# A long convolution whose first transform stage is cut into 32-column groups and turned on chip

## Chip, cores and metric

The kernel runs on one core of one Trainium2 chip. The metric is the device time of one execution in microseconds (us); smaller is better. Three runs of the kernel before gave 924.21 us as their median (921.7 to 927.91). A core has five engines with queues of their own: TensorE (PE in the profile, its weight loads PEld), VectorE (DVE), ScalarE (ACT), GpSimd (POOL) and SyncE (SP), which here issues nearly all DMA transfers. Everything is float32.

## What is computed

```python
def _attn_ref(x, h):                      # x (8, 5696, 128), h (5696, 128)
    L = 2 * S
    Xf = np.fft.rfft(x, n=L, axis=1)
    Hf = np.fft.rfft(h, n=L, axis=0)
    return np.fft.irfft(Xf * Hf[None], n=L, axis=1)[:, :S, :]

def _moe_ref(x, phi, w1, w2):             # x (45568, 128): the result above, flattened
    logits = x @ phi                      # 32 slots: 8 experts of 4
    d = np.exp(logits - logits.max(0)); d /= d.sum(0) + 1e-09
    slot_input = (d.T @ x).reshape(E, S_per_e, D)
    slot_out[e] = np.maximum(slot_input[e] @ w1[e], 0) @ w2[e]       # for each e
    c = np.exp(logits - logits.max(1, keepdims=True)); c /= c.sum(1, keepdims=True) + 1e-09
    return c @ slot_out.reshape(n_slots, D)
```

First a long causal convolution of each of eight sequences with one filter h, channel by channel; then a layer of soft slots, whose slot inputs are weighted over all 45,568 tokens, so that no output row can be written before all tokens are through the convolution.

## The kernel before

The convolution is a transform of length 5760 = 90 x 64 (N1 = 90, N2 = 64) in two stages, a product with the filter's transform, and two stages back. "Image" g = 0 is the filter h, images 1 to 8 are the sequences.

**Stage A** (`load_x`, `fold`, `stage_a`). An image is read in eight chunks of 2 x 4 of the 64 residues. GpSimd folds a chunk with its mirror into a sum and a difference (L201); each of these is multiplied by two tables (L212: 128 columns, of which 90 are used, by 512), ScalarE copies the product out of PSUM into `fst` (L214), and two DMAs store it in DRAM as F (L218), 1 KB per run. That is 32 products per image.

**Stage B** (`load_g`, `stage_b1`, `stage_b2`). The second stage needs the 64 residues on the partitions, so F is loaded back turned (`gt`, L236). A unit is up to four frequencies of each half: 8 matmuls of 64x64 weights by 256 columns, both parts of 128 channels (L250), into `bt`; two multiplications by the filter's transform, Hr and Hi (L270; for h itself by the table `turn`, and the result becomes Hr, Hi); a sum and a difference (L279, on VectorE, in some steps one on GpSimd); `stage_b2` takes the way back (L294), ScalarE copies (L299), and a DMA stores z in DRAM (L302), 1 KB per run. There are 12 units per image: 11 full ones and one with a single frequency of each half.

**Stage C**, per pair T, four of them per image, 32 in all. `load_pair` loads a quarter of an image's z (`zc`, one buffer, two DMAs, L330). `stage_c1` makes the last transform stage: four products of two 64-column matmuls each (L349), ScalarE copies the odd ones, VectorE forms sums and differences (`fold_out`, L354 and L355), GpSimd the last four (`after`, L368). `stage_c2` transposes the 16 blocks (L377), `stage_c3` makes the logits (L386), `column_max` a running maximum per slot (L397 to L405), `stage_c4` transposes the logits and takes the row maximum (L415 to L431), `stage_c5` transposes the exponentials (L438), `softmax` normalises the rows, `dispatch` adds to the slot inputs `acc` (L462, L467), and `stage_c6` stores the weights for the end (`c_t`).

**Order.** The order is written out by hand; the loop at L563 runs over steps t of one chunk of A each. B runs LAG_B = 9 steps behind A, C another 18 behind B, a pair every second step, its parts spread over five steps. Every engine takes its instructions in the order in which this loop issues them. The short-lived products of A and C share a ring of four PSUM banks (L154); `bt` and `bz` have two banks each. When the last unit of B is out, the front's memory is freed and a second loop (L696) finishes the pairs that are left (27 on), with w1 and w2 loaded beside it. Then come the experts (L764 to L794) and the output, eight images in three groups each (L819 to L836).

Of the kernel before, what the change touches and what calls it, by code (L numbers as in the profile page):

```python
# [10 lines left out]
F32 = mybir.dt.float32  # L11
# [3 lines left out]
PSUM = bass.MemoryType.PSUM  # L15

# [6 lines left out]
def transform_tables(S, N1, N2, CH, X0, F0, F1):  # L23

# [4 lines left out]
    N, R1, HALF, P = N1 * N2, S // N2, N2 // 2, 2 * N2  # L36
    k1 = np.arange(N1)
# [3 lines left out]
    s1 = np.stack([np.cos(a1), -np.sin(a1), -np.cos(a1)], 1)  # L41
    a0 = np.outer(alpha, np.arange(N1 // 2) + 0.5)
    i1 = np.stack([np.cos(a0), -np.sin(a0), -np.cos(a0)], 1)
    NP = N1 // 2
    part = s1
    s1 = np.zeros((P, 3, P))
    for a, p in enumerate((F0, F1)):
        s1[X0:X0 + R1, :, p:p + NP] = part[:, :, a * NP:(a + 1) * NP]
    part = i1[np.arange(N1).reshape(2, NP).T.reshape(-1)]
    i1 = np.zeros((P, 3, N2))  # L50
    for r, n, p in z_blocks(N1):
        i1[p:p + n, :, 0:NP] = part[r:r + n]
# [3 lines left out]
    a2 = m2[None, :, None] * omega[:, None, :]  # L56
    w = np.concatenate([np.cos(a2), np.sin(a2)], 1)
    back = np.arange(N2).reshape(2, HALF // CH, CH).transpose(1, 0, 2).reshape(-1)
    NU = (NP + 1) // 2
    turn = (N1 - 1) / 2 * alpha[:, None] + (N2 - 1) / 2 * omega  # L60
    wq = np.zeros((2, N2, NP, N2))
    vq = np.zeros((2, N2, NU, 2, N2))
    tn = np.zeros((2, N2, 2, (NU + 1) // 2, 2, 2))
    for a in range(2):
        wq[a] = w[a * NP:(a + 1) * NP].transpose(1, 0, 2)
        for q in range(NP):
            vq[q % 2, :, q // 2, a] = w[a * NP + q][back].T
            tn[q % 2, :, 0, q // 4, a, q // 2 % 2] = np.cos(turn[a * NP + q]) / N
            tn[q % 2, :, 1, q // 4, a, q // 2 % 2] = np.sin(turn[a * NP + q]) / N
    wq, vq, tn = [t.reshape(P, *t.shape[2:]) for t in (wq, vq, tn)]  # L70
    return [np.ascontiguousarray(t, dtype=np.float32) for t in (s1, i1, wq, vq, tn)]
# [3 lines left out]
def kernel(  # L75
# [13 lines left out]

# [11 lines left out]
    NU = (NP + 1) // 2  # L111
    NW = (NU + 1) // 2
# [4 lines left out]
    NQ = NJ // 2  # L117
    assert S == R1 * N2 and R1 == N1 - 1 and D == P and CH == Q == 4
    SPLIT = R1 // 16 * 16
    X0, F0, F1 = 20, 6, 82  # L120
    ctx.enter_context(tc.manual_schedule())

    t_s1, t_i1, t_w, t_v, t_turn = [
        nc.inline_tensor(t, f"tab_{n}").ap()
        for n, t in zip(("s1", "i1", "w", "v", "turn"), transform_tables(S, N1, N2, CH, X0, F0, F1))]
    fd = [nc.dram_tensor(f"f_{g}", (2, N2, NP, 2, D), F32, kind="Internal").ap() for g in range(B + 1)]
    zd = [nc.dram_tensor(f"z_{b}", (NP, 2 * N2, 2, D), F32, kind="Internal").ap() for b in range(B)]
# [26 lines left out]
    rings = [mid.enter_context(tc.tile_pool(name="ps", bufs=4, space=PSUM))]  # L154
    bps = front.enter_context(tc.tile_pool(name="bps", bufs=1, space=PSUM))
    fconst = front.enter_context(tc.tile_pool(name="fconst", bufs=1))
    lead = ExitStack()
    apool = lead.enter_context(tc.tile_pool(name="apool", bufs=2, side="right"))
    bpool = front.enter_context(tc.tile_pool(name="bpool", bufs=1))

    s1 = apool.tile([P, 3, P], F32, name="s1", tag="s1", bufs=1)
    wt = fconst.tile([P, NP, HP], F32, name="wt")
    vt = fconst.tile([P, NU, 2, HP], F32, name="vt")
    turn = fconst.tile([P, 2, NW, 2, 2], F32, name="turn")
    Hr = fconst.tile([P, NW, 2, 2, D], F32, name="Hr")
    Hi = fconst.tile([P, NW, 2, 2, D], F32, name="Hi")

    def bank():
        rings.append(rings.pop(0))
        return rings[-1].tile([P, 512], F32, name="bank", tag="bank")  # L170
# [5 lines left out]
    for t_ in xcs:  # L176
        nc.vector.memset(t_[:, :, :, :], 0.0)

    def load_x(c):
        if c >= (B + 1) * NJ:  # L180
            return
        g, j = divmod(c, NJ)
# [683 lines left out]
```

## Time and profile before

| | us |
|---|---|
| runs: median (lowest to highest) | 924.21 (921.7 to 927.91) |
| profiled execution, its span | 922.1 |
| VectorE's first and last addition to `acc` (L467) begin at | 237.0, 843.3 |
| first and last product on `zc` (L349) begin at | 182.6, 817.5 |
| SP's issues of x (L190), first and last of the sequences, at | 33.8, 643.7 |

| group | busy us | times |
|---|---|---|
| PE L212, stage A | 275.9 | 576 records, 288 products |
| PE L250, L294, stage B | 116.4, 104.9 | 1620, 1440 records |
| PE L349, stage C1 | 117.1 | 480 records |
| DVE L270 (full, by Hr and by Hi) | 107.4, 106.9 | 88, 88 |
| DVE L279 (full) | 141.4 | 150 |
| ACT L214, copies of stage A | 171.9 | 288 |
| POOL L201, folds | 192.8 | 144 |

DMA moved 272.45 MB in 156,552 packets, 295 GB/s as a mean; 288 stores of F of 180 KB and 99 + 9 loads of F of 512 and 128 KB are among them.

How to read it: busy time counts an engine's instructions without issue or waiting, "records" are the instructions of a group as the profiler lists them (a float32 product is two). Times of matmuls are modelled at their ends, so spacings of their starts say more than their lengths. In the rows, out<-in name what is written and read, the number after "x" is a count, and after the bar stand the busy time in all, the mean of one in ns, and idle time before the group with what ended it.

### The profile page before, as it was taken

What the parts mean: (1) busy time and instruction counts of PE and PEld (TensorE: products, weight loads), DVE (VectorE), ACT (ScalarE), POOL (GpSimd) and SP (SyncE); (2) the same over time, 40 slices, a digit from 0 to 9 for tenths busy, and PEclk for the clock granted to TensorE, in tenths of its full rate; (3) what the DMA queues carried; (4) which work ended last, traced back from release to release, by engine and by line L of the source; (5) the groups of instructions that cost most, each with busy time, mean ns of one, the idle gap of its engine ahead of it and who ended that gap; (6) DMA issues with size and microseconds to landing.
All of it is one profiled execution on the core that took longest, in us unless ns stands there. A gap on an engine that the chain in (4) does not pass through costs nothing.

```text
span 922.1 us, 19325 instructions
## 1 busy us (share of the span) xinstructions
PE 818.0 (89%) x7220; PEld 423.9 (46%) x7220; DVE 653.1 (71%) x887; ACT 481.7 (52%) x888; POOL 488.1 (53%) x426
## 2 busy tenths in 40 slices
PE   6968898899999999999999999999987777878893
PEld 2323344345444445544554454444444434345783
DVE  3047665478888878888888788988887775674552
ACT  4623454455556655555666666656553344475442
POOL 4648766546655565556565655655466552472000
PEclk9989999899999999999999999999999888798865
DMA  9989999999899999999999999999989887761798
GB/s 298 279 274 299 272 345 311 289 345 327 268 320 319 314 282 324 316 314 285 341 304 327 289 324 329 297 318 320 316 269 330 272 254 198 211 249 73 272 405 341
DMA packets 156552, 272.45 MB, mean 295 GB/s; under 512 B 11766, under 2 KB 114422, under 8 KB 153317
## 3 DMA queue, kind: packets, MB, share of 16 engines
q1 hardware_dynamic: 155883, 270.85, 91.4%
q8 instruction: 58, 0.95, 0.4%
q10 hardware_dynamic: 576, 0.36, 0.2%
q14 instruction: 35, 0.29, 0.1%
HBM read 142.86 MB, written 128.21 MB: 294 GB/s over the span
## 4 chain that ended last, share of the span: by engine, by line
PE 51%; DMA 31%; POOL 5%; DVE 5%; issue 3%; SPq 2%; ACT 2%; DVEq 0%; POOLq 0%; ACTq 0%
PE bank L212 17%; DMA zc<-z 11%; PE bank L349 9%; DMA gt<-f 8%; PE bt L250 7%; PE bz L294 6%; DMA out_dram<-o 4%; PE bank L377 4%; DVE p L270 2%; POOL y L368 2%; DMA f<-fst 2%; PE bank L462 2%; DMA z<-zst 2%; PE bank L438 2%; PE bank L386 2%
## 5 line engine op out<-in xcount | busy, mean ns | idle before, releaser
L212 PE MATMUL bank<-x,s 128*128 128x512 f32 x576 | 275.9, 614 | 12.3 <-POOL x L201 12.0
L201 POOL TENSOR_TENSOR x<-xc 128x512 f32<-128x512 f32 x144 | 192.8, 1342 | 154.7 <-PE bank L212 70.4
L214 ACT ACTIVATE fst<-bank 128x512 f32<-128x512 f32 x288 | 171.9, 597 | 95.5 <-PE bank L212 74.8
L299 ACT ACTIVATE zst<-bz 128x1024 f32<-128x1024 f32 x96 | 93.2, 971 | 205.4 <-PE bz L294 198.5
L270 DVE TENSOR_TENSOR p<-bt,Hr 128x1024 f32<-128x1024 f32 x96 | 112.9, 1176 | 108.0 <-PE bt L250 95.7
L212 PEld LDWEIGHTS bank<-x,s 128*128 128x128 f32 x576 | 102.4, 193 | 131.5 <-issue 93.4
L279 DVE TENSOR_TENSOR yf<-p 128x512 f32<-128x512 f32 (+1 forms) x163 | 146.4, 931 | 3.3
L250 PE MATMUL bt<-gt,wt 64*64 64x256 f32 x1620 | 116.4, 394 | 25.1 <-DMA gt<-f 22.0
L349 PE MATMUL bank<-zc,i 128*64 128x512 f32 x480 | 117.1, 610 | 7.0 <-DMA zc<-z 4.1
L294 PE MATMUL bz<-yf,vt 64*64 64x256 f32 x1440 | 104.9, 393 | 15.5 <-POOL yf L279 15.0
L270 DVE TENSOR_TENSOR p<-bt,Hi 128x1024 f32<-128x1024 f32 x96 | 112.3, 1170 | 0.0
L250 PEld LDWEIGHTS bt<-gt,wt 64*64 64x64 f32 x1620 | 55.0, 134 | 102.0 <-issue 31.6
L368 POOL TENSOR_TENSOR y<-y,op 128x512 f32<-128x512 f32 x64 | 77.5, 1211 | 7.8 <-DVE op L354 5.1
L294 PEld LDWEIGHTS bz<-yf,vt 64*64 64x64 f32 x1440 | 58.2, 137 | 44.2 <-POOL yf L279 21.0
L279 POOL TENSOR_TENSOR yf<-p 128x512 f32<-128x512 f32 (+1 forms) x29 | 45.9, 1583 | 53.9 <-DVE p L270 53.9
L368 POOL TENSOR_TENSOR y<-y,om 128x512 f32<-128x512 f32 x54 | 71.8, 1330 | 2.1
L270 DVE TENSOR_TENSOR p<-bt,turn 128x1024 f32<-128x1024 f32 (+1 forms) x24 | 27.2, 1174 | 57.8 <-PE bt L250 57.7
L349 PEld LDWEIGHTS bank<-zc,i 128*64 128x64 f32 x480 | 30.8, 138 | 68.3 <-issue 40.8
L377 PE MATMUL bank<-ident,y 109*128 109x109 f32 x512 | 60.0, 275 | 0.7 <-DVE y L368 0.7
L377 PEld LDWEIGHTS bank<-ident,y 109*128 109x128 f32 x512 | 53.5, 151 | 13.6 <-issue 11.9
L379 ACT ACTIVATE yt<-bank 128x360 f32<-128x360 f32 x128 | 50.9, 482 | 3.3 <-PE bank L377 3.3
L819 PE MATMUL op<-so,cT 32*128 32x128 f32 x704 | 46.0, 374 | 4.4 <-ACT o L828 3.6
(97 smaller groups left out, 851.5 us busy)
## 6 DMA issues: line engine op xcount, KB each, us to landing
f<-fst SPq DMA_DIRECT2D x288, 180.0 KB
gt<-f SPq DMA_DIRECT2D x99, 512.0 KB
z<-zst SPq DMA_DIRECT2D x88, 512.0 KB
zc<-z SPq DMA_DIRECT2D x30, 1024.0 KB
xc<-in_x_dram SPq DMA_DIRECT2D x64, 320.0 KB
out_dram<-o SPq DMA_DIRECT2D x16, 1024.0 KB
zc<-z SPq DMA_DIRECT2D x30, 416.0 KB
out_dram<-o SPq DMA_DIRECT2D x8, 768.0 KB
```

Of the source, the lines that this page charges most:

```text
L201: nc.gpsimd.tensor_tensor(out=y_[:, :, :], in0=t_[:, 0, :, :], in1=t_[:, 1, ::-1, :], op=AL.subtract if comp else AL.add)
L212: nc.tensor.matmul(p[:, :], s1[:, tab[G], :], src[:, :, :].rearrange("p n d -> p (n d)"), start=True, stop=True)
L214: nc.scalar.activation(st[:, :, G, :], p[:, :].rearrange("p (n d) -> p n d", d=D), AF.Copy)
L250: nc.tensor.matmul(bt[q * HP:(q + 1) * HP, a, o, :], wt[r, 2 * i + q, :], t_[r, 2 * o + q, :, :].rearrange("p c d -> p (c d)"), start=True ...
L270: nc.vector.tensor_tensor(out=p_[r, 0:k, :, :], in0=pv, in1=h_, op=AL.mult)
L279: eng.tensor_tensor(out=y_[r, 0:k, c, :], in0=pr[r, 0:k, c, :], in1=pi[r, 0:k, 1 - c, :], op=op_)
L294: nc.tensor.matmul(bz[a * HP:(a + 1) * HP, q, o, :], vt[r, i, a, :], y_[r, a * m + o, :, :].rearrange("p c d -> p (c d)"), start=True, sto ...
L299: nc.scalar.activation(st[:, 0:m, 0:n, :].rearrange("p o q x -> p q o x"), bz[:, 0:n, 0:m, :], AF.Copy)
L349: nc.tensor.matmul(p[h_ * HP:(h_ + 1) * HP, :], i1[0:kr, tab, :], t_[0:kr, h_, o, :, q, :], start=True, stop=True)
L368: eng.tensor_tensor(out=part_, in0=part(v, 0), in1=o_[:, :, :], op=sign)
L377: nc.tensor.transpose(p[:, i * TR:(i + 1) * TR], ys[T][0:TR, k * CH + i, 0:D], ident[0:TR, 0:TR])
L379: nc.scalar.activation(yt[:, k * CH:(k + 1) * CH, :, :], of_tokens(p), AF.Copy)
```

## The change

The first stage leaves no F in DRAM, and half of the channels (64) are worked on at a time; there are 18 such halves H, nine images of two. A half is loaded as eight DMAs into one tile X[dh] of two, with 256 bytes per run. GpSimd folds it in place, in four steps j of two operations.

`stage_a(H, k)` makes eight products: 32 columns of the table each, by 32 residues x 16 channels, in two groups of four that write the four 32-partition quarters of one tile `pa` (two PSUM banks, one buffer). Table columns are ordered so that a quarter holds 32 frequencies of one kind (even or odd below 64 for k = 0 to 3, the 26 others for k = 4, 5) and one part. VectorE then turns `pa` by one transposition of 32x32 blocks into F1 or F3, which have the residues on the partitions, and `stage_b1` reads them at once.

A half has six units of stage B: four of 16 matmuls of 128 columns, one of 32 and one of 20 of 64 columns. The two multiplications now write `pi` and, in place, `bt` in PSUM, and both sums are on VectorE, with one operand in `bt`. `bt`, `bz`, `pa` and `pi` have one buffer each. z is stored in runs of 512 bytes.

In stage C the parts are placed by unit: a pair takes three units (STARTS), with `stage_c1` cut in two. Its PSUM ring has two banks while the front runs, eight after it. The running maximum is one reduction, since ScalarE no longer overwrites the unused column, which holds LOWEST; the difference of maxima goes into the exponential as its bias. The front now holds 28 pairs, so the closing loop begins at pair 28. Tables change with the layout.

```diff
@@ memory
-    rings = [mid.enter_context(tc.tile_pool(name="ps", bufs=4, space=PSUM))]
+    banks = [front.enter_context(tc.tile_pool(name="ps", bufs=2, space=PSUM))]
+    aps = front.enter_context(tc.tile_pool(name="aps", bufs=1, space=PSUM))
     bps = front.enter_context(tc.tile_pool(name="bps", bufs=1, space=PSUM))
...
+    F1 = bpool.tile([P, 32, 2, HD], F32, name="F1")
+    F3 = bpool.tile([P, 32, 2, 32], F32, name="F3")
+    X = [apool.tile([P, N2 + 8, HD], F32, name=f"X{i}") for i in range(2)]
+    NH = 2 * (B + 1)
@@ loading and folding
+        for n0 in (0, 48, 16, 32):
+            for r in (slice(0, SPLIT), slice(SPLIT, R1)):
+                nc.sync.dma_start(out=X[dh][r, 8 + n0:24 + n0, :],
+                                  in_=src[r, n0:n0 + 16, dh * HD:(dh + 1) * HD])
...
+        for op_, dst in ((AL.add, t_[0:R1, 8 * j:8 * j + 8, :]),
+                         (AL.subtract, t_[0:R1, hi:hi - 8:-1, :])):
+            nc.gpsimd.tensor_tensor(out=dst, in0=t_[0:R1, lo:lo + 8, :],
+                                    in1=t_[0:R1, hi:hi - 8:-1, :], op=op_)
@@ stage A
-            nc.scalar.activation(st[:, :, G, :],
-                                 p[:, :].rearrange("p (n d) -> p n d", d=D), AF.Copy)
-            nc.sync.dma_start(
-                out=fd[g][a, n0:n0 + CH, :, :, :].rearrange("n q c d -> q n (c d)"),
-                in_=st[p:p + NP, :, :, :].rearrange("k n c d -> k n (c d)"))
...
+        p = aps.tile([P, 2, 512], F32, name="pa", tag="pa")
+        for c in range(2):
+            for q in range(4):
+                a, comp = divmod(q, 2)
+                d0 = 16 * k if k < 4 else 16 * (k - 4) + 32 * a
+                nc.tensor.matmul(p[32 * q:32 * q + 32, c, :],
+                                 s1[0:R1, comp + c, a if k < 4 else 2, :],
+                                 t_[0:R1, 40 * comp:40 * comp + 32, d0:d0 + 16],
+                                 start=True, stop=True)
+        def turn():
+            f_ = F1[:, :, :, 16 * k:16 * k + 16] if k < 4 else \
+                F3[:, :, :, 16 * (k - 4):16 * (k - 4) + 16]
+            nc.vector.transpose(f_.rearrange("p k c d -> p c d k"),
+                                p[:, :, :].rearrange("p c (n d) -> p c d n", d=16))
@@ stage B
+        o0, no = (0, 4) if i < 4 else (0, 8) if i == 4 else (8, 5)
+        for o in range(no):
+            for a in range(2):
+                r = slice(a * HP, (a + 1) * HP)
+                for par in range(2):
...
+                    nc.tensor.matmul(bt[par * HP:(par + 1) * HP, a, o * w_:(o + 1) * w_], l_,
+                                     m_.rearrange("p c d -> p (c d)"), start=True, stop=True)
...
+        for dst, f_ in ((iv, fs[1]), (pv, fs[0])):
+            if i == 5 or g == 0:
+                for c in range(2):
+                    nc.vector.tensor_tensor(out=dst[:, :, :, c, :], in0=pv[:, :, :, c, :],
+                                            in1=f_[c], op=AL.mult)
+            else:
...
+                nc.vector.tensor_tensor(out=m(dst), in0=m(pv), in1=w_.broadcast_to([P, 2 * no, 2, dn]),
+                                        op=AL.mult)
+            for c, op_, dst in outs:
+                nc.vector.tensor_tensor(out=dst, in0=pv[:, :, :, c, :], in1=iv[:, :, :, 1 - c, :],
+                                        op=op_)
@@ order
+    NU = 6 * NH
+    STARTS = {12 * (T // NQ + 2) + 2 + 3 * (T % NQ): T for T in range(NT - NQ)}
+    for n in range(NU + 3):
+        H, i = divmod(n, 6)
+        T, ph = STARTS.get(n - (n - 2) % 3), (n - 2) % 3
...
+        turns = [(H + 1, 0)] if i == 3 else [(H + 1, 1)] if i == 4 else \
+            [(H + 1, 2), (H + 1, 3)] if i == 5 else [(H, 3 + i)] if i else []
+        sums = stage_b1(n) if n < NU else lambda: None
+        if turns:
+            stage_a(*turns.pop(0))()
+        sums()
+        if 0 < n <= NU:
+            stage_b2(n - 1)
+        if turns:
+            stage_a(*turns.pop(0))()
+        if i == 3:
+            load_x(H + 2)
+        if K is not None:
+            if ph == 0:
+                if K >= 1:
+                    stage_c3(K - 1)
+                if K >= 2:
+                    dispatch(K - 2)
+                if T is not None:
+                    state[T] = stage_c1(T)
+                    state[T][0]()
+                if K >= 1:
+                    column_max(K - 1)
+            elif ph == 1:
+                if K >= 2:
+                    stage_c6(K - 2)
+                if K >= 1:
+                    stage_c4(K - 1)
+                if T is not None:
+                    _, second, after = state.pop(T)
+                    second()
+                    after()
+                    if (T + 1) % NQ or T == V:
+                        load_pair(T + 1)
+            else:
+                if K >= 1:
+                    stage_c5(K - 1)
+                    softmax(K - 1)
+                if T is not None:
+                    stage_c2(T)
...
+        if i in (5, 0, 1, 2):
+            fold(H + 2 if i == 5 else H + 1, (i + 1) % 6)
```

## Prediction

> **What bounds the kernel now.** First the page: busy time by engine, then its 40 slices.
>
> ```profile
> PE 818.0 (89%) x7220; PEld 423.9 (46%) x7220; DVE 653.1 (71%) x887; ACT 481.7 (52%) x888; POOL 488.1 (53%) x426
> ...
> PE   6968898899999999999999999999987777878893
> ...
> DVE  3047665478888878888888788988887775674552
> ...
> DMA  9989999999899999999999999999989887761798
> ```
>
> TensorE is above 90% in nearly every slice from the ninth to the 29th, VectorE is next, and the DMA engines are full. Next the busy time in two stretches of 100 us (TensorE, weight loads, VectorE, ScalarE, GpSimd, clock, DMA share, GB/s):
>
> ```profile
> 300.00:400.00 100.00, 97.48 (x894) 49.77 (x893) 82.84 (x112) 59.62 (x110) 57.25 (x50) 1.00 0.99 308
> 400.00:500.00 100.00, 96.89 (x826) 47.88 (x825) 85.75 (x115) 59.43 (x110) 56.65 (x51) 1.00 0.98 313
> ```
>
> TensorE has 3% to spare, VectorE 15%. The chain of waits names transfers for 31% of the span, but beside them TensorE works on, so I take TensorE as the bound here and full transfers as a near second. Now TensorE's timeline over one pair T, and VectorE's beside it:
>
> ```profile
> 550.48 1.09 PE L250 MATMUL bt<-gt,wt 64*64 64x256 f32 x16
> 551.39 1.04 PE L294 MATMUL bz<-yf,vt 64*64 64x256 f32 x16
> 552.37 1.98 PE L212 MATMUL bank<-x,s 128*128 128x512 f32 x4
> ...
> 554.89 1.94 PE L349 MATMUL bank<-zc,i 128*64 128x512 f32 x8 [0.54 <-DMA zc<-z]
> ...
> 565.12 1.09 PE L462 MATMUL bank<-y,d 128*32 128x129 f32 x32
> ...
> 568.03 1.71 PE L377 MATMUL bank<-ident,y 109*128 109x109 f32 x16
> ```
>
> ```profile
> 551.64 1.23 DVE L270 TENSOR_TENSOR p<-bt,Hr 128x1024 f32<-128x1024 f32 x1 [2.54 <-PE bt L250]
> 552.78 1.22 DVE L270 TENSOR_TENSOR p<-bt,Hi 128x1024 f32<-128x1024 f32 x1
> 554.03 1.29 DVE L279 TENSOR_TENSOR yf<-p 128x512 f32<-128x512 f32 x2
> ...
> 557.01 0.69 DVE L354 TENSOR_TENSOR y<-bank,y 128x512 f32<-128x512 f32 x1
> ```
>
> I take spacings of starts as prices. TensorE: one unit of the second stage (8 matmuls, 256 columns) 0.91; its way back 0.98; two first-stage products 1.72; half of stage_c1 1.87; dispatch 1.02; stage_c2 1.58; and from the same view stage_c3 0.74, a four-transposition group 0.55 to 0.6. VectorE: a 1024-wide multiplication out of PSUM 1.14 to 1.22, a 512-wide sum with one PSUM operand 0.69; two sums from SBUF 1.29 here, 0.976 each on average over the run. stage_c2 repeats every 22 us (548 to 570 is such a pair), so a half image, two pairs, takes 43.75 us (87.5 per image).
>
> **First stage.** Per image 32 products of 128 columns by 512 go (27.5 us of TensorE) and 24 groups of four 32-column products of 512 columns come. The price of such a group is in the trace:
>
> ```profile
> L764 PE MATMUL bank<-w1s,siz 128*32 128x512 f32 x32 | 3.6, 595 | 0.3 <-DVE siz L754 0.3
> ...
> L785 PE MATMUL bank<-w2s,hidT 128*32 128x128 f32 x128 | 3.7, 273 | 0.0
> ```
>
> L764 has 32 records, two per product: 16 products, 4 groups, 3.6 us, 0.9 a group beside 0.86 for one full product now. So 24 groups are 20.9 us: 6.6 us less per image. That the groups read X at a stride has no row; the bounds are 0.86 and the 3.4 of four products in turn, and L764 is nearest.
>
> **Second stage.** The columns streamed are the same, in smaller matmuls: 232 instead of 90 per image in stage_b1 (128 of 128 columns, 104 of 64), 180 instead of 90 in stage_b2. L785 prices a 128-column one at 3.7/64 = 0.058 us, which is its share of 0.91 too (0.91/16 = 0.057); so units of 16 stay at 0.92, and I see no cost there. For 64 columns nothing is shown: bounds 0.029 (half) and 0.067 (two weight loads; 55.0 us over 1,620 loads is 0.034 each). I take 0.058, the nearest row: 32 of them 1.86, 20 of them 1.16. That adds about 3 us per image.
>
> **VectorE.** It gains 108 transpositions of 128x1024 out of PSUM. Nearest row: 1.22 (same size, same source). Bounds: 0.69, and 2.44 if a block's filling and emptying do not overlap. [...] VectorE also takes all second-stage sums (GpSimd had 26), but each now has one operand in PSUM: 0.69 instead of 0.976. Two part reductions become one (0.5 less), df goes (0.2 less). The multiplication in place in PSUM I price at 1.22 too.
>
> **ScalarE, GpSimd.** 171.9 us of fst copies go from ScalarE and a second stage_c3 copy (0.48) comes per pair; GpSimd loses 46 us. Neither was the bound: nothing counted. The folds are 144 of 512 as before, on the same queue, ahead of use by two units.
>
> **Transfers.** 288 stores and 108 loads of F go, with 104 of 272 MB. But x now comes in 256-byte pieces (5,696 per half) and z goes in 512-byte ones (5,760 per half). The nearest row is ScalarE's queue at the start, whose packets average 0.21 MB/386 = 544 bytes:
>
> ```profile
> q10 hardware_dynamic: 386, 0.21, 38.6%
> ```
>
> 38.6% of 16 engines over 2 us is 12.35 us, 32 ns a packet. Bounds: 10.6 ns (256 bytes at the 24 bytes/ns of the closing output) and 86.5 ns (the run's mean packet: 91.4% x 16 x 922/155,883). At 32 ns a half needs 182 + 184 + 122 (zc, 2.95 MB at 24) + 43 (c_t, and completion packets at the upper bound), over 16: 33 us of engine time, below the 47 found next. [...] On SP's queue eight x issues (0.47 each by the same line now) stand ahead of a zc load in unit 3 below: x takes 11 us, zc 4 and about 2 of latency, and unit 5 needs it some 2 us later still. I count nothing; every 10 ns more per x packet would cost 3.6 us there.
>
> **The order.** The freed time only counts if the queues allow. Per half, TensorE now needs 40.05 us and VectorE 39.75 (my sums by unit below), both under 43.75. But bt, pa, bz and pi have one buffer each, and the pairs' stages two PSUM banks instead of four: stage_b1 of unit n+1 waits for the sums of n, a turn for its products, the next products for that turn. Laid out with the prices above, from one multiplication's start to the next unit's (unit: VectorE, TensorE, result):
> - 0: 5.7, 4.5, 5.7. VectorE bound.
> - 1: 6.15, 5.8, 6.65. stage_c2 ends at 5.5 (GpSimd's four sums, two banks), then stage_b1 and its latency, 1.15.
> - 2: 7.25, 7.25, 9.1. Multiplications, turn and sums to 4.8, acc to 5.0; only now is dispatch's bank free for the second c1 product: ready 6.85; its two sums to 8.25; maximum and low 0.85.
> - 3: 6.8, 6.6, 7.05. c1 to 5.0, then 32 small matmuls, 1.86 plus latency.
> - 4: 6.15, 6.7, 7.55. stage_c2 to 6.2, then 1.16 plus latency.
> - 5: 7.7, 9.2, 11.0. The second group needs pa, free after the first turn at 3.05; its turn ends at 6.1; stage_c3 and dispatch are queued behind it on TensorE to 6.65; acc, product, sums to 10.1; maximum and low.
>
> Sum 47.05 us per half, 3.3 more than now: the time that waited beside TensorE's full queue now alternates with it.
>
> **The sum.** Start: 33 us, estimated as 16 until the last piece of x lands (3.5 MB with the tables, at the first slices' rate and after 2 us), half of the folds behind it (4 of 1.27), and four times 1.75 + 1.2. h: 12 units without pairs, 4.9 + 1.16 each by the same rules, with split multiplications 79. First image's 14 units: 86. So the first pair starts at 198 (182.6 now). 81 units to pair 27: 13.5 x 47.05 = 635; no products in the last three, -4; its own three units and what follows, 21. The first pair of the tail then starts at 850. Now:
>
> ```profile
> 767.84 1.94 PE L349 MATMUL bank<-zc,i 128*64 128x512 f32 x8
> ...
> 804.69 1.94 PE L349 MATMUL bank<-zd,i 96*64 96x512 f32 x8 [1.56 <-DMA zd<-z]
> ...
> 813.74 1.94 PE L349 MATMUL bank<-zc,i 128*64 128x512 f32 x8
> ```
>
> Here it starts at 767.84 and 154.3 us remain. The changed tail has one pair fewer, 9.05 by the two lower rows: 145. Total 995 by the span. The 64-column price is the term that I trust least, and its lower bound lies further off: at 0.029 it takes 1.5 us off each half, 20 in all; I take a third of that, 7. The span is then 988, and the time 990, since the runs' median lies 2.1 above the profiled 922.1.
>
> **Rivals.** (a) *The queues interlock better than I laid them out*, VectorE never waits: 39.75 per half, 13.5 x 7.3 = 99 less, 896. It decides from about 42 per half, where the time equals 924. For it: both engines' sums lie under the present period, and transfers get slack. Against: each wait above follows from one buffer. 0.15. (b) *The turn costs 2.44*: 108 x 1.22 = 132 more, 1120. No row speaks for it, none excludes it. 0.1. (c) *Small packets bind*: past 51 ns per packet a half's transfers exceed 47 us; at 60 they take 53.3, and 16.5 halves x 6.2 give 1092. 0.07. That it leaves F in DRAM is excluded: the diff has no store or load of F left.
>
> **How the numbers follow.** The forecast has 0.68 and, by bounds of small terms, some 950 to 1030. A measurement of this kernel tells about 1%, 915 to 933, from no change. Faster 0.15, (a) without its upper edge; same 0.06, its edge and the forecast's lower flank; slower 0.79. The range takes in most of (a) and half of (b): 900 to 1070.
>
> **What would show it.** Right: a half near 47 us, TensorE's share of the middle near 85% and VectorE's also, TensorE waiting for VectorE at stage_b1 and at c1's second product; DMA share near 75%; turns at 1.2. Wrong: VectorE over 95% there (a), turns over 2 us (b), DMA full with GpSimd or TensorE waiting for x or z (c).

## The result and the profile after

The changed kernel takes 1078.78 us, the median of four runs (1075.27 to 1081.84), beside 926.06 us for the kernel before in the same session: a ratio of 1.1626, 95% interval 1.1562 to 1.1689. The forecast was 990 us with a range of 900 to 1070, so the sign was right and the time lies above the range. The profiled execution has a span of 1073.3 us, 85 more than the 988 of the forecast. Line numbers from here on are those of the changed kernel: L216 the products of stage A, L224 the turn, L249 `stage_b1`, L272/L277 its multiplications, L291 the sums, L310/L321 `stage_b2`, L379 the products of `stage_c1`.

From the page of the changed kernel, TensorE's busy time, then TensorE, VectorE and the granted clock in the 40 slices of the span (27 us each):

```profile
PE 828.1 (77%) x12368; PEld 455.5 (42%) x12368; DVE 784.3 (73%) x1025; ACT 338.0 (31%) x661; POOL 408.1 (38%) x387
...
PE   0655557676888888887988888888888888896893
DVE  1275656666878789888988888898888989484442
...
PEclk9975555867889999999999999999999999896865
```

The middle is what the forecast said, both engines at 7 to 9 tenths, mostly 8. The third to the tenth slice are not: TensorE and VectorE are at 5 to 7 tenths, both, and the granted clock falls to 5 tenths. Two stretches show the difference (TensorE, weight loads, VectorE, ScalarE, GpSimd, clock, DMA share, GB/s):

```profile
100.00:200.00 100.00, 65.24 (x788) 29.74 (x782) 62.38 (x72) 4.10 (x4) 14.47 (x12) 0.59 0.28 51
400.00:500.00 100.00, 85.63 (x1418) 47.39 (x1414) 85.47 (x113) 38.82 (x77) 47.62 (x44) 1.00 0.65 159
```

Set beside the forecast's own steps, the spans divide like this:

| | forecast | measured | difference |
|---|---|---|---|
| start, to the first `stage_b1` | 33 | 51.4 | +18 |
| h, 12 units | 79 | 105.0 | +26 |
| first image, 14 units, to the first pair (L379) | 86 | 118.2 | +32 |
| sum of these three: the first pair begins at | 198 | 274.6 | +76 |
| from there to the tail's first pair | 652 | 659.8 | +8 |
| what remains | 145 | 138.9 | -6 |
| taken off for cheaper 64-column products | -7 | | +7 |

Nine tenths of the miss lies ahead of the first pair, in a stretch in which only stages A and B run. TensorE's timeline there, in units of h (start, length, what; in brackets the idle time before and what ended it), and VectorE's over the same units:

```profile
110.03 1.99 PE L249 MATMUL bt<-F,wt 64*64 64x128 f32 x32 [4.29 <-DVE H1i L291]
111.95 3.64 PE L216 MATMUL pa<-X,s 89*32 89x512 f32 x16
118.81 1.98 PE L249 MATMUL bt<-F,wt 64*64 64x128 f32 x32 [3.22 <-DVE H1i L291]
```

```profile
112.08 1.29 DVE L272 TENSOR_TENSOR pi<-bt,t 128x512 f32<-128x512 f32 x2 [2.19 <-PE bt L249]
...
115.66 1.89 DVE L224 STREAM_TRANSPOSE F<-pa 128x1024 f32<-128x1024 f32 x1 [0.83 <-PE pa L216]
...
118.00 0.67 DVE L291 TENSOR_TENSOR H1i<-bt,pi 128x512 f32<-128x512 f32 x1
120.85 1.29 DVE L272 TENSOR_TENSOR pi<-bt,t 128x512 f32<-128x512 f32 x2 [2.19 <-PE bt L249]
```

Three things are to be seen. The two engines wait for each other in turn: VectorE for `bt` and for `pa`, TensorE for VectorE's last sum. TensorE's work takes twice its later time: L249 spaced 1.92 where 1.03 is the price beside the pairs, L216 3.6 where it is 1.85. And the turn takes 1.89 us (1.97 as a mean over the run), not 1.22. A unit with one turn takes 8.8 us here. The forecast had laid out 6.06 for it, and 6.6 as a mean of h's 12 units with their split multiplications (79 us); their measured mean is 8.7.

The experiments ask how much of the 76 us each of these is, and whether the 47 us that a half takes beside the pairs came about as the forecast reasoned. Two readings are given for each: when the first pair begins, and the length of a half (mean of the twelve halves from the sixth to the seventeenth, from the first multiplication of one to that of the next; 47.75 us in the changed kernel, its shortest 46.6).

### The profile page after: what moved, and what is told of

Read it like the earlier page. It is cut to its first block, busy times and chain, and to the rows that moved or that the text cites. A ratio compares the mean times of both kernels' runs of the same rounds, so it can differ in the third digit from the quotient of the medians.

```text
span 1073.3 us, 28430 instructions
## 1 busy us (share of the span) xinstructions
PE 828.1 (77%) x12368; PEld 455.5 (42%) x12368; DVE 784.3 (73%) x1025; ACT 338.0 (31%) x661; POOL 408.1 (38%) x387
## 4 chain that ended last, share of the span: by engine, by line
PE 28%; DVE 26%; DMA 19%; POOL 10%; ACT 3%; issue 3%; SPq 2%; DVEq 0%; POOLq 0%; ACTq 0%
DMA zc<-z 15%; PE pa L216 9%; POOL y L401 8%; DVE F L224 6%; PE bank L379 6%; PE bt L249 6%; DVE y L291 4%; DMA out_dram<-o 4%; DVE pi L277 3%; DVE bt L277 3%; POOL L L460 2%; PE bank L410 2%; DVE y L385 2%; DVE y L386 2%; SPq L189 2%
## 5 line engine op out<-in xcount | busy, mean ns | idle before, releaser
L216 PE MATMUL pa<-X,s 89*32 89x512 f32 x1728 | 248.9, 698 | 51.8 <-POOL X L202 27.4
L224 DVE STREAM_TRANSPOSE F<-pa 128x1024 f32<-128x1024 f32 x108 | 212.2, 1965 | 81.5 <-PE pa L216 81.4
L202 POOL TENSOR_TENSOR X<-X 89x512 f32<-89x512 f32 x144 | 183.2, 1273 | 197.7 <-DMA X<-in_x_dram 173.0
L379 PE MATMUL bank<-zc,i 128*64 128x512 f32 x480 | 119.6, 618 | 42.8 <-DMA zc<-z 22.8
L249 PE MATMUL bt<-F,wt 64*64 64x128 f32 x2304 | 94.2, 310 | 56.1 <-DVE y L291 24.2
L249 PEld LDWEIGHTS bt<-F,wt 64*64 64x64 f32 x2304 | 74.4, 152 | 107.4 <-issue 70.0
L216 PEld LDWEIGHTS pa<-X,s 89*32 89x32 f32 x1728 | 49.9, 120 | 162.2 <-issue 94.4
L291 DVE TENSOR_TENSOR y<-bt,pi 128x512 f32<-128x512 f32 x192 | 115.5, 640 | 0.7
L277 DVE TENSOR_TENSOR pi<-bt,H1i 128x1024 f32<-128x1024 f32 x64 | 78.0, 1219 | 26.3 <-PE bt L249 26.3
L310 PEld LDWEIGHTS bz<-y,vt 64*64 64x64 f32 x2048 | 58.9, 139 | 56.8 <-issue 56.8
L277 DVE TENSOR_TENSOR bt<-bt,H1r 128x1024 f32<-128x1024 f32 x64 | 78.2, 1222 | 0.0
L310 PE MATMUL bz<-y,vt 64*64 64x128 f32 x2048 | 75.0, 287 | 0.0
L379 PEld LDWEIGHTS bank<-zc,i 128*64 128x64 f32 x480 | 30.5, 138 | 94.5 <-issue 39.0
L249 PE MATMUL bt<-F,wg 64*64 64x64 f32 x1872 | 39.8, 238 | 24.9 <-DVE y L291 11.2
```

Of the source, the lines that this page charges most:

```text
L202: nc.gpsimd.tensor_tensor(out=dst, in0=t_[0:R1, lo:lo + 8, :], in1=t_[0:R1, hi:hi - 8:-1, :], op=op_)
L216: nc.tensor.matmul(p[32 * q:32 * q + 32, c, :], s1[0:R1, comp + c, a if k < 4 else 2, :], t_[0:R1, 40 * comp:40 * comp + 32, d0:d0 + 16], ...
L224: nc.vector.transpose(f_.rearrange("p k c d -> p c d k"), p[:, :, :].rearrange("p c (n d) -> p c d n", d=16))
L249: nc.tensor.matmul(bt[par * HP:(par + 1) * HP, a, o * w_:(o + 1) * w_], l_, m_.rearrange("p c d -> p (c d)"), start=True, stop=True)
L277: nc.vector.tensor_tensor(out=m(dst), in0=m(pv), in1=w_.broadcast_to([P, 2 * no, 2, dn]), op=AL.mult)
L291: nc.vector.tensor_tensor(out=dst, in0=pv[:, :, :, c, :], in1=iv[:, :, :, 1 - c, :], op=op_)
```

## Experiments on the time ahead of the pairs

**Keeping TensorE busy.** The two banks of the pairs stand unused before the first pair. `e1_warm` puts products into them that nothing reads:

```diff
+    def warm(n, v):
+        p = bank()
+        for _ in range(n):
+            nc.tensor.matmul(p[:, :], ident[0:v.shape[0], :], v, start=True, stop=True)
...
+        if n < 26:
+            warm(2, ident[:, :].unsqueeze(1).broadcast_to([P, 4, P]))
         if i == 3:
             load_x(H + 2)
```

> Adds products of 128x512 whose results nothing reads, in the two banks that stand unused before the first pair: two per unit in the 26 units before it, six while the first folds run, one after each of the four turns of the start. Clock theory: ahead of the pairs TensorE is idle in each unit, its granted clock is 0.5 to 0.6, and so the second stage's products (1.04 us instead of about 0.5 to 1.0) and the groups (1.85 instead of 0.9) stand on the path between VectorE's steps. Then the clock there goes above 0.9, the units of h go from 8.8 to about 7.2 us, the first pair from 274.6 to 220-240 us, and the time falls by 35 to 60 us. Turn theory (the turn of 1.8 to 1.97 us instead of 1.22 is what lengthens the units): a change of at most 10 us either way. Loads theory (256-byte pieces of x come late): no change.

Measured: 1040.81 us, ratio to before 1.1214 [1.1124, 1.1304], 38 us less than the changed kernel; the first pair at 242.3 instead of 274.6 us; the half 47.56. From 60 to 150 us the granted clock is 0.88, beside 0.58 in the changed kernel. First the changed kernel, then `e1_warm`:

```profile
60.00:150.00 90.00, 54.42 (x576) 21.92 (x568) 58.73 (x75) 0.00 (x0) 20.27 (x16) 0.58 0.23 33
60.00:150.00 90.00, 68.82 (x724) 26.83 (x724) 65.85 (x81) 0.00 (x0) 20.31 (x16) 0.88 0.23 34
```

Doing more on TensorE made the kernel faster. Its timeline:

```profile
108.23 1.10 PE L254 MATMUL bt<-F,wt 64*64 64x128 f32 x32
109.27 1.92 PE L216 MATMUL pa<-X,s 89*32 89x512 f32 x16
111.12 1.98 PE L232 MATMUL bank<-ident 128*128 128x512 f32 x4
115.21 1.10 PE L254 MATMUL bt<-F,wt 64*64 64x128 f32 x32 [2.10 <-DVE H1i L296]
```

The products are back at 1.04 and 1.85, and the unit is at 7.0 us.

The control leaves the extra products in place and takes their work away (`p[:, 0:16]`, 16 columns of `ident` instead of 512):

> The control of e1_warm: the same extra products at the same places, but of 16 columns instead of 512, so that TensorE is hardly busier. Nothing reads them. Clock theory: the granted clock ahead of the pairs stays at 0.5 to 0.65, the first pair at 268 to 280 us and the time within 10 us of the changed kernel's. If it was the order or the waits that the extra products brought and not the clock, this kernel gains as e1_warm did, 25 us or more.

```profile
60.00:150.00 90.00, 63.40 (x612) 29.88 (x604) 57.53 (x74) 0.00 (x0) 20.24 (x16) 0.71 0.22 33
```

That is the same stretch of the control. Its clock reads 0.71, but this record reads 1.00 until 90.7 us, while the products there already take twice their later time. Their lengths say it better: from 60 to 220 us, 88% of the records of stage A (L216) are at half speed (1.06 us, where 0.59 is the length beside the pairs) in the control, 77% in the changed kernel and 12% in `e1_warm`. The first pair of the control is at 283.1 and its time 1080.85 us (ratio 1.1647 [1.159, 1.1705]). Nothing is gained, so it was not an order or a wait that the extra products brought. The small products are not free either (four records take 1.04 us at half speed), so against its control `e1_warm` gains 41 us ahead of the first pair, and 32 against the changed kernel.

Is it idle time, or are the narrow products of the new stages too small to count? `e15_narrow` writes the extra products into `p[0:32, :]`, with 32 columns of weights:

> The extra products of e1_warm at the same places and as many columns each, but into 32 of the array's 128 columns; nothing reads them. Idle theory (the clock falls because TensorE stands idle in each unit): as long as they keep TensorE as busy, the gain is that of e1_warm, the first pair at 238 to 248 us. Width theory (narrow products, such as the first stage's 89x32 and the second's 64x64, count less for the clock than full ones): the clock ahead of the pairs stays at 0.5 to 0.7 and the first pair at 268 us or later, though TensorE's busy share rises as in e1_warm.

```profile
60.00:150.00 90.00, 65.81 (x760) 23.92 (x755) 65.34 (x81) 1.02 (x1) 20.30 (x16) 0.91 0.25 39
```

Clock 0.91, first pair 237.4, one time of 1034.81 us: the narrow ones do at least as well. The width theory falls. And three full ones per unit instead of two:

> e1_warm with three extra products per unit ahead of the pairs instead of two; nothing reads them. If the clock there was still partly low with two (0.85 to 0.90 in the record), three bring it to 0.95 or more, the halves of h go from 44.7 to 42.5 us and the first pair from 242 to 232-238 us. If 0.9 is all there is to gain, the first pair stays at 240 to 245, or comes later by the products' own time (up to 0.9 us a unit, 20 us).

First pair 243.1, one time of 1041.89 us, clock 0.95 from 50 to 150 us. A third product brings no more; whether its own time eats what the clock still gains is not shown. Two bring 32 us of the 76, net of their own time.

**The turn.** `e3_copy` puts `nc.vector.tensor_copy` in place of the transposition, with the same patterns; `e4_contig` keeps the transposition and lets it read and write one run of 1024; `e5_sides` does so on one side at a time:

```diff
-            f_ = F1[:, :, :, 16 * k:16 * k + 16] if k < 4 else \
-                F3[:, :, :, 16 * (k - 4):16 * (k - 4) + 16]
-            nc.vector.transpose(f_.rearrange("p k c d -> p c d k"),
-                                p[:, :, :].rearrange("p c (n d) -> p c d n", d=16))
+            f_ = F1[:, 8 * k:8 * k + 8, :, :] if k < 4 else \
+                F3[:, 16 * (k - 4):16 * (k - 4) + 16, :, :]
+            nc.vector.transpose(f_.rearrange("p k c d -> p (k c d)"),
+                                p[:, :, :].rearrange("p c x -> p (c x)"))
```

> The turn is a plain VectorE copy with the same source and destination patterns, so F is not transposed within its blocks. Turn theory: the copy takes about 1.2 us, and most of 108 x 0.66 = 71 us goes: 50 to 75 us less, the units ahead of the pairs about 0.7 us shorter. Clock theory: the first pair comes 15 to 20 us earlier, and beside the pairs part of it is hidden behind TensorE: 20 to 45 us less. If the patterns and not the operation are what is slow, the copy takes 1.8 to 2 us too and nothing changes.

> The turn's transposition reads pa and writes F as one run of 1024 elements, so its blocks lie in another order than the products need. If the strides (64 bytes in pa, 512 bytes in F) make the turn slow, it takes about 1.2 us and the time falls as with the copy; if it is the operation, it stays at 1.8 to 2 us and the time within 10 us of the changed kernel's.

> The turn's two sides are measured apart, in one kernel: in the four turns of a half that fill F1 the source keeps its 64-byte stride and the destination is one run; in the two that fill F3 the source is one run and the destination keeps its stride. The blocks then lie in another order than the products need. If reading pa at 64 bytes is what costs 0.7 us of the turn, the F1 turns stay near 1.95 us and the F3 turns take about 1.24; if writing F at a stride does, it is the other way round; if both share it, both lie at 1.5 to 1.6. On the time: within 15 us of the changed kernel's either way.

The groups of the turn (shortest, median, longest in ns, first and last start) in the changed kernel, then with the copy, with one run on both sides (the diff above), and by sides (L224 writes one run, L229 reads one):

```profile
L224 DVE STREAM_TRANSPOSE F<-pa x108: 1892/1966/2046, 32.4 to 894.5; 128x1024 f32<-128x1024 f32 x108
```

```profile
L224 DVE COPY F<-pa x108: 1867/1947/2020, 31.8 to 901.3; 128x1024 f32<-128x1024 f32 x108
```

```profile
L224 DVE STREAM_TRANSPOSE F<-pa x108: 1236/1240/1252, 32.4 to 876.2; 128x1024 f32<-128x1024 f32 x108
```

```profile
L224 DVE STREAM_TRANSPOSE F<-pa x72: 1237/1241/1251, 32.7 to 860.1; 128x1024 f32<-128x1024 f32 x72
L229 DVE STREAM_TRANSPOSE F<-pa x36: 1893/1988/2047, 59.5 to 880.5; 128x1024 f32<-128x1024 f32 x36
```

The transposition itself costs what the forecast took, 1.24 us; a plain copy with its patterns is as slow as the turn. It is the destination, one float every 512 or 256 bytes in F1 and F3, that costs 0.7 us (1.966 beside 1.240; 1.988 for F3 alone, whose source is one run); the source's stride of 64 bytes in PSUM costs nothing (1.241). The times: 1082.10 us with the copy (ratio 1.1676 [1.1565, 1.1787], as the changed kernel), and single times of 1058.31 with one run on both sides, first pair 247.3, and 1060.56 by sides, first pair 254.0.

The starts here are 1.16 and 1.81 us apart for 1024 columns, 1.13 and 1.77 ns a column: the destination's steps of 128 and 64 words make the difference of 0.65 us. The forecast had taken its 1.22 from the row of a multiplication of the same size and had not asked about the stride.

`e13_warm_contig` joins the extra products and the turn in one run:

> The extra products of e1_warm (read by nothing) and the turn in one run of 1024 elements on both sides, so F's blocks lie in another order than the products need. Ahead of the pairs VectorE is then the path: 28 turns at 0.6 us less give 17 us, so the first pair at 222 to 230 us (242.3 with the extra products alone), and if the turn's length does not count beside the pairs, the halves there stay at 46.5 to 47 at best and the time falls by 12 to 20 us to 1020-1030. If it counts there too, another 0.6 us for each of 80 turns, 48 us, goes: below 990.

One time of 1023.98 us. The first pair comes at 218.7, another 23.6 us earlier; the units of h take 6.4 us and its 12 units 77.6, where the forecast had 79. So with clock and destination mended h is as long as forecast, and the two account for 56 of the 76 us. Of the other 20, 12 are the start and 4 a wait of the first pair for its `zc`, which the forecast did not have (it is 0.6 in the changed kernel, where everything else is later).

**The turn's stride moved to TensorE.** `e8_dn_order` reads X channel by channel, so that `pa` is written in the turn's order:

```diff
-                                 t_[0:R1, 40 * comp:40 * comp + 32, d0:d0 + 16],
+                                 t_[0:R1, 40 * comp:40 * comp + 32, d0:d0 + 16].rearrange("p n d -> p d n"),
```

> The first stage's products read X in the order channel, position (256 bytes from one element of a row to the next), so that pa is written channel by channel and the turn reads it as one run; F is written as before, and the output is the reference's. If the turn's source is its slow side, the turn falls from 1.95 to about 1.25 us; if TensorE reads at the stride for nothing, a group pair stays at 1.85 us, the first pair comes 20 to 27 us earlier as with the turn in one run, and the time falls by 15 to 25 us. If TensorE pays for the stride, its groups take 2 us or more and the gain is lost or reversed. If the destination is the slow side, nothing changes.

1375.04 us (ratio 1.4787 [1.4716, 1.4859]). A pair of groups, 1.85 us before, in this kernel:

```profile
608.49 5.54 PE L216 MATMUL pa<-X,s 89*32 89x512 f32 x16
```

TensorE pays threefold for a moving operand with 256 bytes between elements, and the turn stays at 1.97, since its slow side is the destination. Nor does TensorE alone pay. VectorE beside this pair of groups:

```profile
608.56 2.19 DVE L386 TENSOR_TENSOR om<-bank,om 128x512 f32<-128x512 f32 x1
610.53 2.54 DVE L277 TENSOR_TENSOR pi<-bt,H3Ai 128x1024 f32<-128x1024 f32 x1
```

In the changed kernel these take 0.69 and 1.21, also while stage A's products run. GpSimd's folds, 1.27 there, take up to 3.65 here. So the half, which goes from 47.75 to 67.16, 19.4 more, pays for 3.62 us in each of six pairs of groups (21.7 us of TensorE) and for slower neighbours as well: this run doesn't price TensorE's work beside the pairs.

**The start.** In `e1_warm` six of the extra products stood behind the folds and ran at half speed. `e16_warm_start` (which also has all that helped, see below) runs 28 products on the identity while x is loaded:

> e10_together with the extra products of the start moved: 28 full-width ones on the identity run while x is loaded, from 2 to about 26 us, in place of the six behind the folds, which ran at half speed for 10.6 us and held the first group back by 2.5 us. If the half-speed groups of the start (3.64 us, where 1.85 is the later price) are a matter of the clock, the groups of the start take 1.9 us, the first stage_b1 comes at 42 to 45 us instead of 49.7, and the time falls by 4 to 8 us to 1008-1014. If the start is held by something else, no change.

First `e1_warm`, then `e16_warm_start`:

```profile
19.48 10.61 PE L232 MATMUL bank<-X,ident 89*128 89x512 f32 x12 [19.48 <-POOL X L202]
30.02 3.64 PE L216 MATMUL pa<-X,s 89*32 89x512 f32 x16
```

```profile
1.37 26.69 PE L232 MATMUL bank<-ident 128*128 128x512 f32 x56 [1.37 <-POOL one L135]
27.99 1.92 PE L216 MATMUL pa<-X,s 89*32 89x512 f32 x16
```

All four pairs of groups of the start now take 1.92, and `stage_b1` first runs at 43.9 us, beside 49.7 in `e10_together`, from which this run differs in the extra products of the start alone. From the first group on it is 15.9 us instead of the changed kernel's 24.0. So the start's slow groups went as well when TensorE was busy ahead of them (3.64 us to 1.92). That this is the clock is the author's reading of the lengths: in the changed kernel the record reads 1.00 there.

## Experiments on the order beside the pairs

**Sums ahead of the turn.** In `e2_sums_first` the turn is issued after `sums()` in all units, so that `bt` is free earlier:

```diff
-        if turns:
-            stage_a(*turns.pop(0))()
-        sums()
+        turn = stage_a(*turns.pop(0)) if turns else lambda: None
+        sums()
+        turn()
```

> VectorE's two sums go ahead of the first turn of a unit. Buffer theory (the single bt tile keeps stage_b1 of the next unit waiting for sums that stand behind a turn): bt is free 1.8 us earlier, stage_b1 runs beside the turn, VectorE's wait of 2.19 us per unit ahead of the pairs goes in the units with a turn (about 20 of 26, 35-40 us) and the 26 us of such waits beside the pairs go in part: 45 to 70 us less. Turn theory: VectorE's own work is the path, in whatever order: at most 15 us less. Clock theory: 15 to 45 us less, ahead of the pairs alone.

1065.01 us (1.147 [1.1393, 1.1547]), 14 less. Ahead of the pairs it does what the buffer theory says, first pair at 241.2, and TensorE's shorter idle times come with a better clock there (55% of stage A's records at half speed, not 77%), so the 33 us are not the order's alone. Beside them the half grows to 49.75, since unit 5 takes 13.7 to 15.3 us in most halves instead of mostly 11.5 to 12.6: its second group waits for the first turn (TensorE's waits for turns rise from 11.6 to 21.6 us between 310 and 860). `e7_warm_sums` keeps the old order in unit 5 and adds the extra products:

> The extra products of e1_warm (read by nothing), and VectorE's sums ahead of the turn except in unit 5 of each half. Clock and buffer theories together: ahead of the pairs a unit takes 5.4 to 5.9 us instead of 7.0, the halves of h 37 to 40 us instead of 44.7, the first pair comes at 210 to 228 us (242.3 with the extra products alone), and since unit 5 keeps its order the halves beside the pairs stay at 46.5 to 49: the time is 1005 to 1027 us. If it was the sums' place in the other units that lengthened e2_sums_first beside the pairs, the halves there take 49 to 51 us and the time stays at 1035 or above.

1030.36 us (1.107 [1.1001, 1.1139]); units of 5.8 us, first pair at 225.9, half 47.99.

**What TensorE waits for.** TensorE's waits in the changed kernel from 310 to 860 us (total, times, longest), the five longest of seven:

```profile
PE bank L379 <- DMA zc<-z: 18.6, 16, 1.9
PE bank L410 <- ACT d L470: 17.5, 23, 0.8
PE bank L379 <- ACT cst L525: 15.2, 23, 1.0
PE pa L216 <- DVE F L224: 11.6, 11, 1.1
PE bank L410 <- POOL y L401: 7.2, 23, 0.3
```

All seven make 78.0 us of 550, 14%, and TensorE is busy for the other 86%: 41 us of work and 6.8 of waits per half. The turn is in 1 us of these. VectorE is as busy (477 us beside TensorE's 471), so the shares don't say which of the two is the path. Nor does the chain of work that ended last, in the same stretch:

```profile
by line: DMA zc<-z 24.2%; POOL y L401 13.7%; PE bank L379 8.2%; PE pa L216 4.7%; DVE y L291 4.7%; DVE bt L277 4.6%; DVE pi L277 4.5%; DVE F L224 4.1%; PE bt L249 3.4%; POOL L L460 3.1%; issue 2.9%; DVE y L385 2.8%; DVE y L386 2.8%; PE bz L3
```

It runs through transfers of `zc`, GpSimd, TensorE and VectorE by turns. Three kernels each work on one wait. `e6_banks` lets `bz`'s two banks join the ring of the pairs (`bufs=4`, `bz = [bank(), bank()]`, ScalarE empties each by itself):

> Four rotating banks shared by the pairs' stages and the second stage's way back (bz's two banks join the ring, ScalarE empties each by its own instruction), in place of two for the pairs and one two-bank bz. Bank theory (beside the pairs the half of 47 us is set by TensorE waiting for one of two banks): TensorE's waits for cst, lt and d ahead of the pairs' products go, unit 2 falls from 8.9 to under 8 us and unit 5 by 1 us or more, a half takes 43 to 45.5 us, and the time falls by 20 to 50 us. TensorE theory (its own 40 us of work and the alternation with VectorE set the half): a half stays at 46.5 or above, and the time within 10 us. Clock theory of the start: the first pair stays at 270 to 276 us.

1075.50 us (1.155 [1.1486, 1.1614]). The waits for cst and d are gone, and the shortest halves fall from 46.6 to 45.6-46.0; but waits of `stage_b1` for the sums rise from 5.6 to 22.7 us in the same window, and the mean half is 47.49. The bank theory had the waits right and their worth wrong.

`e9_zc_first` moves `load_x(H + 2)` behind the pair's parts of the same unit. In the changed kernel its issues, eight and not 16, hold SyncE's queue for 7 to 10 us, ahead of the pair's load:

```profile
427.99 9.08 SPq L189 DMA_DIRECT2D X<-in_x_dram  x8
```

> In unit 3 of each half the 16 issues of x go behind the pair's load on SP's queue instead of ahead of it. Queue theory (the zc load comes late for unit 5 because x's issues and transfers stand ahead of it): unit 5 of a half falls from 11.5-12.6 to about 11 us, its spread goes, TensorE's wait for zc of 22.8 us falls to under 12, and the time falls by 6 to 14 us. Order theory (unit 5 is set by its two turns, the second group and one bank): unit 5 stays at 11.5 or above and the time within 5 us. If the x loads then come late for the folds, the time rises by 5 to 20 us. The first pair stays at 270 to 276 us either way.

1070.14 us (1.1537 [1.1472, 1.1602]). The wait for `zc` falls from 22.8 to 10.5 us over the run, unit 5 is 11.5 in nearly every half, and the gain of 8.6 is the queue theory's. What is left of the wait is all in unit 2 of an image's first half, where `load_pair` comes right after the image's last z store.

`e12_less_dispatch` keeps only `i = 0` of the products of a sum in `dispatch`:

> Leaves out three of four products of each sum in dispatch, 12 of 16 per pair, so the slots' inputs lack three quarters of the tokens. TensorE does 0.75 us less per pair, VectorE and ScalarE the same. TensorE theory (beside the pairs TensorE's own work and its waits are the path): a half is 1.0 to 1.5 us shorter and the time 14 to 22 us less. VectorE theory (the path runs through VectorE and TensorE has slack): a half changes by less than 0.5 us and the time by less than 7 us.

1094.11 us (1.1784 [1.1695, 1.1872]): slower, against both theories. In unit 2:

```profile
424.37 1.94 PE L379 MATMUL bank<-zc,i 128*64 128x512 f32 x8 [1.90 <-DVE acc L496]
```

The products of `stage_c1` now wait for the addition to `acc`, which stands on VectorE behind the turn and the sums; in the changed kernel they wait 0.34 for ScalarE's `lt`. Unit 2 takes 9.7 us or more instead of 8.9. Why the banks come free in that order was not followed up, so this run says nothing on how much TensorE's work counts.

**Together.**

> What helped, together: the extra products that nothing reads, sums ahead of the turn except in unit 5, four shared banks, x's issues behind the pair's load, and the folds of the first half of h shared between VectorE and GpSimd by channels. If the parts add up: the first pair at 195 to 212 us (start 5 us earlier), a half beside the pairs at 44.5 to 47 us, and the time between 985 and 1015 us. If beside the pairs one bound takes the other's place (TensorE's wait moves from the banks to bt, as the shared banks alone showed), a half stays at 46 to 48 and the time at 1012 to 1028.

1017.96 us (1.095 [1.0868, 1.1033]), first pair 229.5, half 47.18: in the range of one bound taking the other's place, above that of full addition, and with the first pair later than the 195 to 212 expected (the start, 49.7 us, gained 1.7, not 5). With the start kept busy (`e16_warm_start` above) it is 1008.36 (1.0855 [1.0761, 1.0949]), the best of all versions and still 8.6% slower than the kernel before.

## Why the prediction was wrong

*The direction* was right: with single buffers the two engines wait for each other, the kernel is slower, and a half takes about 47 us with both at 85 to 88%.

*The step that failed* is "Start: 33 us", "h: 12 units without pairs, 4.9 + 1.16 each", "First image's 14 units: 86. So the first pair starts at 198": 274.6 was measured. The mechanism, alternation, was the right one; its terms were sized wrongly. TensorE's terms came from rows beside the pairs, where TensorE is 97% busy and the clock 1.00. Without pairs the alternation itself leaves TensorE idle in every unit, the granted clock falls to 0.59 (100 to 200 us), and most of its steps, which stand on the path there, take twice as long: 32 us by `e1_warm`, 41 against its control. VectorE's term was the turn, 1.22 taken and 1.81 measured by spacing, 24 us ahead of the first pair by `e13_warm_contig`. The rest, some 20, is not split by a run in full. The trace shows the start's eight folds from 18.05 to 28.7 us, where half of them were to be done by 16, and its four groups 5.7 us apart, where 2.95 was taken; most of that went when TensorE was kept busy ahead of them: `e16_warm_start` has them 3.9 to 4.1 apart.

*The half of 47.05* agreed with 47.75 (46.6 the shortest), but the terms did not, so the agreement is in part luck. The layout put the turn on the path in units 1 to 5; six turns of 1.81 would then have made it 50.6. In `e4_contig` and `e13_warm_contig` the six turns are 3.9 us shorter together, and the half is 48.38 and 47.88, no shorter. The trace shows where a part of the gain goes: TensorE's waits for `zc` rise from 18.6 to 30.9 us in `e4_contig` (310 to 860), and its shortest halves, less that wait, are 45.4 us beside 46.3 to 46.6. So about 1 of the 3.9 us could show if `zc` came in time; a run of both was not made. The waits that the forecast named as signs are not the ones that came, either: TensorE's wait for VectorE at `stage_b1` is 5.6 us of the 78, and the products of `stage_c1` wait for ScalarE and `zc`, not for VectorE. What sets the half is open. No experiment shortens TensorE's work beside the pairs without lengthening a wait, and those on single waits gain 0.3 us per half (`e6_banks`) and 9 us in the whole time (`e9_zc_first`). The 64-column products cost 0.034 each (1.09 for 32 of them), near the lower bound; that took 1.2 us off each half (1.86 less 1.09, 1.16 less 0.74), and the waits for `zc`, for which the forecast had counted nothing, gave 1.6 back (18.6 us in 550). It had put the eight issues of x at 0.47 each; they hold the queue for 7 to 10 us.

*Rivals.* (a) did not occur: VectorE is at 85 to 88% in the middle. (b) was half right in price (1.81 by spacing, between 1.22 and 2.44) and wrong in place: 108 x 0.6 = 65 us, had every turn been on the path; it cost 24 ahead of the first pair and nothing that a half shows. (c) is excluded: x's 256-byte packets took 29.3 ns each (5,796 packets in 17.7% of 16 engines over the 60 us from 60 on), beside the 32 assumed, and TensorE waits for a fold only once, at the start. The DMA share of the middle is 0.65 to 0.67, not 0.75. Two sums were off and changed little: (a)'s 896 is taken from 995, and from 990 it is 891; 24 groups at 0.9 are 21.6 us, not 20.9, and 22.2 at the 1.85 per pair of groups measured.

*What was missing* was the question in which state a row's price was taken. The trace of before has no stretch in which TensorE alternates with VectorE: before its first pair stage A kept TensorE 85% busy at a clock of 0.97:

```profile
50.00:150.00 100.00, 85.21 (x588) 36.75 (x592) 63.20 (x64) 41.40 (x64) 70.60 (x49) 0.97 0.95 301
```

Its rows were no price for a stretch of alternation alone, and the forecast set no bound for that.

The stretch that the forecast needed had idle times of 2 to 4.3 us between TensorE's groups and a granted clock of 0.58 (60 to 150 us of the changed kernel). The kernel before has products at half speed at its start: the first four records of stage A's products, which start from 8.2 to 11.0 us, are 1.06 us long or more, and from 12.3 us on they are mostly 0.59. `e1_warm` shows that products without a pause did not always end it: those from 19.5 to 30 us stayed at half speed.

## What to carry over

A price taken beside the pairs, where TensorE was 97% busy, did not hold here where it was 65% busy (100 to 200 us): ask of each stage what keeps TensorE busy while it waits, and add as a bound the sum with its products at twice their length (here 3.6 us a pair of groups, beside 1.85) if nothing does. For a VectorE operation ask for the stride of its destination as well as its size; here the stride cost 0.7 us, more than the operation's kind (1.947 us for a copy, 1.966 for the transposition). And where a forecast agrees in one number, look at whether the terms agree as well.

## What was not expected of the hardware

- Products that nothing reads made the kernel 38 us faster, and it did not matter whether they filled 128 or 32 columns of the array (1040.81 us, and a single time of 1034.81).
- The granted clock in the record reads 1.00 up to 64.6 us (90.7 in the control), while the products there take twice their later time (records of 1.06 us, 0.59 later); only their lengths show it.
- Six products on rows of X ran at half speed for 10.6 us without a pause (e1_warm); 28 products of as many columns each, on the identity from the start on (e16_warm_start), ran at full speed after 5 us (56 records in 26.69 us). Why is open.
- A moving operand with 256 bytes from element to element takes TensorE about three times as long (5.47 us against 1.85 by spacing), and makes instructions of VectorE beside it slower too (2.19 and 2.54 us above, 0.69 and 1.21 in the changed kernel). A source with 64 bytes in PSUM costs VectorE nothing (1.241 us), and a destination with 256 or 512 bytes in SBUF costs it 0.7 us (1.966 in the changed kernel).
